# Nine of 49 exponentials on VectorE, taken two at a time, a plan with a lock between VectorE and GpSimd, and another layout for the horizontal results

## The chip, the cores and the metric

The kernel runs on one core of a Trainium2 chip. The metric is the device time of one execution in microseconds. Five engines work side by side, each through a queue of its own in order: TensorE (PE in the profile, PEld for its weight loads), ScalarE (ACT), VectorE (DVE), GpSimd (POOL), and SyncE (SP), whose queue here issues all DMAs. They meet at semaphores.

## The reference

Window attention in two directions on one 224 x 224 image with 96 channels, bfloat16. The first 48 channels attend inside horizontal stripes of 8 rows, the last 48 inside vertical stripes of 8 columns; each stripe is a window of 1792 tokens, and there are 28 + 28 of them. Then one projection of all channels.

```python
def reference(x, wqkv, wo):
    B, H, W, C = x.shape                       # 1, 224, 224, 96
    sw = 8; C2 = C // 2; nh, nw = H // sw, W // sw
    qkv = jnp.einsum('bhwc,cd->bhwd', x, wqkv)
    q, k, v = qkv[..., :C], qkv[..., C:2*C], qkv[..., 2*C:]
    scale = C2 ** (-0.5)
    # horizontal: channels :C2, windows of 8 rows x 224
    ah = softmax(einsum('bqc,bkc->bqk', qh, kh) * scale); oh = einsum('bqk,bkc->bqc', ah, vh)
    # vertical: channels C2:, windows of 224 x 8 columns
    av = softmax(einsum('bqc,bkc->bqk', qv, kv) * scale); ov = einsum('bqk,bkc->bqc', av, vv)
    return jnp.einsum('bhwc,cd->bhwd', concat(oh, ov), wo)
```

## The kernel before

Two windows are done together: a pass `P`. Passes 0 to 13 are horizontal, 14 to 27 vertical. In a pass the 1792 queries are cut into four chunks (512, 512, 512, 256), and each chunk's scores into units of 128 x 1024 (a key tile of 128 by 512 queries by two windows; two key tiles in the chunk of 256). There are 49 units in a pass. For each unit PE makes the scores into one of three PSUM slots of two banks (`qk`, the pool `ring`), an engine makes exponentials of them in SBUF, and PE multiplies these with V and adds them up in one of two further banks (`pv_op`, `obanks`).

- 41 units of a pass go to ScalarE (`add_a`): one `activation` into `PT`, one product with V.
- 8 units go to VectorE (`add_d`; `NDC` says how many of each chunk). Its exponential is built from four instructions of 1024 elements a partition: `I_sb` (the shifted score as int16, the only one that reads PSUM, and it frees the slot), `U_sb` and `E_sb` (fraction and exponent bits, int16 to int16), and `G_sb` (a product of two bf16 tensors). E and G are each multiplied with V, so such a unit has two products.

Around the units, `prep` makes the next pass's K, Q and V from `xT_sb` with `fill`: PE writes a bank, VectorE evicts it. For K the mean over the keys is taken off: VectorE sums it (`kjunk`, `negmean`), and GpSimd subtracts it (`ev3`). When a chunk is complete, VectorE evicts it to `OT_sb` and `fin` projects it: PE, a reciprocal, a product (`d2`). For a horizontal pass `d2` writes `Ph_sb`, which keeps all horizontal results in SBUF. For a vertical pass `d2` writes `tmp`, GpSimd adds `Ph_sb` (`d3`, into `out_sb`), and SP issues one DMA for every 16 x 8 pixels: 28 a pass.

`load` fetches x transposed: 2 DMA transposes for a horizontal pass, 16 of 224 pixels for a vertical one. The load for pass P + 2 goes into the buffer of pass P.

The order is made by a list scheduler (`Planner`) when the kernel is built: each `Op` has an engine, a cost `occ`, a latency, dependencies, buffers to take; each engine has several queues with priorities, and the planner places next what can start first by its costs. What it gives out is a fixed order for every engine, with semaphore waits for the dependencies alone: no start time of the plan is enforced. It reckons 0.06 us of SP's queue for each x load and each output DMA.

Of the kernel before, what the change touches and what calls it, by code (L numbers as in the profile page):

```python
# [218 lines left out]
EPS, HOLD, RUN, BATCH = 0.02, 0.12, 1.5, 2  # L219
PRIO = (1, 0, 3, 5, 4, 2)  # L220
NEAR, LEAD, SPACE, PACE, DRUN = 1, 3, 4, 0.9, 0.9


def bass_standalone__window_attn_cswin__vision_kernel(
# [23 lines left out]
    NPT, NY, NL, NR = 8, 2, 4, 4  # L248

    es = ExitStack()  # L250
    with es:
# [131 lines left out]
        def load(P, stream):  # L383
            b = P % 2
            for w in range(2):
# [10 lines left out]
                for i, (tr, dst, s_) in enumerate(todo):  # L396
                    fn = (lambda e, dst=dst, s_=s_: e.dma_start_transpose(dst, s_)) if tr else \
                         (lambda e, dst=dst, s_=s_: e.dma_start(dst, s_, allow_slow_non_contiguous=True))
                    op = Op("sp", 0.06, 4.0, fn, xt_read.get(P - 2, []) if i == 0 else [], dma=(s_x[b][w], own if i == 0 else 0))
# [162 lines left out]
        ph_ready = {}  # L562
        out_dma = {P: [] for P in range(NP)}

        def fin(P, c):
# [7 lines left out]
            if is_h[P]:  # L573
                bcs = list(range(q0 // 64, (q0 + qs) // 64))
                for i in range(0, len(bcs), 4):
# [16 lines left out]

                    def rel(op, rop=rop):
# [3 lines left out]
                                   ("dve", 0.07 + 0.1 * n, d2, [], True, dve_ev, [], rel)], stream=pe_fin)  # L597
                    rop.append(ops[0])
                    fin_pe[P].append(p)
                    for bc in g:  # L600
                        ph_ready[(P, bc)] = ops[1]
            else:
                kts = list(range(q0 // 128, (q0 + qs) // 128))
                for w in range(2):
                    j = 2 * (P - NPH) + w
                    g, n = kts, len(kts)

                    def pe_fn(e, bk, g=g, n=n, w=w):
# [5 lines left out]
                        return ins
                    hold = []

                    def d2(e, bk, op, n=n, hold=hold):
                        r = rc[hold[0].tok["r"]]
                        return e.tensor_tensor(tmp[op.tok["t"]][:, 0:n, :], bk[:, 0:n * (C + 1)].rearrange("p (s c) -> p s c", s=n)[:, :, 0:C],  # L619
                                               r[:, 0:n].unsqueeze(2).to_broadcast([128, n, C]), ALU.mult)  # L620
# [8 lines left out]
                    def done(op, g=g, w=w, j=j, hold=hold):  # L629
                        tmps.free(hold[1].tok["t"], [op])  # L630
                        for kt in g:
                            dm = Op("sp", 0.06, 2.0, lambda e, kt=kt: e.dma_start(out_v[j, kt], out_sb[b][:, w, kt, :]), [op], dma=(s_out[b], 0))
# [106 lines left out]

        def add_d(u, soft):  # L740
            P, c, kts = u
            b = P % 2
# [7 lines left out]
            d.fn = lambda e: e.tensor_scalar(I_sb[d.tok["y"]][:, :].rearrange("p (s n) -> p s n", s=2), two(q.tok["s"]),  # L750
# [4 lines left out]
            f = Op("dve", 0.334, 0.415, None, [d])  # L755
            f.fn = lambda e: e.tensor_scalar(U_sb[d.tok["y"]][:, :], I_sb[d.tok["y"]][:, :], M_FRAC, HALF, ALU.bitwise_and, ALU.bitwise_or)  # L756
            x2 = Op("dve", 0.334, 0.415, None, [d], [], [(ls, "l", 1)])
            x2.fn = lambda e: e.tensor_scalar(E_sb[x2.tok["l"]][:, :], I_sb[d.tok["y"]][:, :], M_EXP, E_LOW, ALU.bitwise_and, ALU.bitwise_or)  # L758
            g = Op("dve", 0.60, 0.68, None, [f, x2], [], [], lambda op: ys.free(d.tok["y"], [op]))
            g.fn = lambda e: e.tensor_tensor(G_sb[x2.tok["l"]][:, :], I_sb[d.tok["y"]][:, :].bitcast(BF16), U_sb[d.tok["y"]][:, :].bitcast(BF16), ALU.mult)  # L760
            dve_ts.extend([f, x2, g])
            for t, buf in ((x2, E_sb), (g, G_sb)):
                def pv_then(op, t=t):
                    if t is g:
                        ls.free(x2.tok["l"], [op])
                    pv_done(k, op)
                v = pv_op(k, kts, lambda w, kt: V_sb[b][:, w, kt, :],
                          lambda w, i, qs, buf=buf: buf[x2.tok["l"]][:, w * 512 + i * qs:w * 512 + (i + 1) * qs].bitcast(BF16),
                          [t] + v_ready[P], pv_then)
                last_pv[P].append(v)  # L770
                pe_pd.append(v)

        prep(0, startup=True)
# [89 lines left out]
```

## Time and profile before

| | us |
|---|---|
| median of 3 runs (lowest, highest) | 1103.57 (1100.68, 1105.23) |
| the profiled execution | 1103.27 |
| its span, first to last instruction | 1101.5 |
| ACT busy | 1062.8 |
| PE busy | 1046.9 |
| DVE busy | 949.9 |
| POOL busy | 153.3 |

Busy times are unions of what runs on an engine; a matmul's end is modelled, so PE's is no measure of how full it is. The mean time of one instruction in a group is that of its record, and records of neighbours overlap by some hundredths of a microsecond. `L726` and the like are lines of the kernel before. In a timeline the bracket behind a row is the idle time ahead of it and what ended it.

### The profile page before, as it was taken

How to read it: one execution, taken by the hardware profiler on the slowest of the kernel's cores; microseconds unless marked ns; L12 is line 12 of the kernel's file. 1: busy time of each engine (PE TensorE's matmuls, PEld its weight loads, DVE VectorE, ACT ScalarE, POOL GpSimd, SP SyncE). 2: the span in 40 equal slices, each digit the busy share in tenths (PEclk: the TensorE clock that was granted, in tenths of full speed). 3: DMA queues.
4: the chain of work that ended last, by engine and by line, in shares of the span. 5: the costliest groups of instructions: out<-in, count | busy, mean ns of one | idle time of the engine just before them, and what ended most of it. 6: DMA issues, size and time to landing. Idle time of an engine off the chain costs nothing.

```text
span 1101.5 us, 24997 instructions
## 1 busy us (share of the span) xinstructions
PE 1046.9 (95%) x10424; PEld 386.4 (35%) x10424; DVE 949.9 (86%) x1941; ACT 1062.8 (96%) x1154; POOL 153.3 (14%) x143
## 2 busy tenths in 40 slices
PE   7999999999999999999999999999999999989996
PEld 2333333333333333333333333333333333323332
DVE  5899889889888998898899889988988978868876
ACT  4999999999999999999999999999999989979996
POOL 0000000000000000000022122222221222212221
PEclk9999999999999999999999999999999989989998
DMA  5101201110121012011112222222222222222110
GB/s 104 35 1 35 35 9 27 35 35 1 35 35 34 1 35 35 3 33 29 20 29 42 39 41 42 39 41 43 40 41 42 41 39 43 40 39 42 37 29 19
DMA packets 168904, 37.05 MB, mean 34 GB/s; under 512 B 168792, under 2 KB 168792, under 8 KB 168792
## 3 DMA queue, kind: packets, MB, share of 16 engines
q1 hardware_dynamic: 168792, 35.47, 17.5%
q8 instruction: 81, 1.33, 0.5%
q14 instruction: 31, 0.25, 0.1%
HBM read 0.10 MB, written 9.63 MB: 9 GB/s over the span
## 4 chain that ended last, share of the span: by engine, by line
ACT 63%; PE 17%; DVE 17%; issue 1%; DMA 0%; POOL 0%; POOLq 0%; SPq 0%
ACT PT L726 63%; PE ps L708 8%; PE ps L691 7%; DVE I_sb L750 5%; DVE G_sb L760 4%; DVE KT_sb L518 2%; DVE U_sb L756 2%; DVE E_sb L758 1%; DVE OT_sb L655 1%; PE ps L499 1%; PE ps L583 1%; DVE QT_sb L513 1%; DVE Ph_sb L590 1%; DMA xT_sb<-in_x_dram 0%; PE ps L612 0%
## 5 line engine op out<-in xcount | busy, mean ns | idle before, releaser
L726 ACT ACTIVATE PT<-ps 128x1024 bf16<-128x1024 f32 x1148 | 1059.3, 1107 | 20.8 <-PE ps L708 20.1
L708 PE MATMUL ps<-QT_sb,KT_sb 48*128 48x512 bf16 (+1 forms) x3136 | 490.9, 360 | 25.4 <-ACT PT L726 16.0
L691 PE MATMUL ps<-PT,V_sb 128*64 128x512 bf16 (+1 forms) x2576 | 447.6, 371 | 0.3 <-ACT PT L726 0.3
L750 DVE TENSOR_SCALAR I_sb<-ps 128x1024 int16<-128x1024 f32 x224 | 273.4, 1221 | 42.7 <-PE ps L708 37.7
L708 PEld LDWEIGHTS ps<-QT_sb,KT_sb 48*128 48x128 bf16 x3136 | 125.1, 93 | 327.8 <-ACT PT L726 195.6
L691 PEld LDWEIGHTS ps<-PT,V_sb 128*64 128x64 bf16 x2576 | 134.1, 108 | 170.4 <-issue 160.4
L760 DVE TENSOR_TENSOR G_sb<-I_sb,U_sb 128x1024 bf16<-128x1024 bf16 x224 | 176.9, 790 | 3.3
L623 POOL TENSOR_TENSOR out_sb<-tmp,Ph_sb 128x384 bf16<-128x384 f32 (+1 forms) x112 | 99.8, 896 | 414.4 <-DVE tmp L619 338.9
L529 POOL TENSOR_SCALAR KT_sb<-KT_sb,negmean 128x1792 bf16<-128x1792 bf16 x27 | 53.3, 1976 | 529.8 <-DVE kjunk L523 529.7
L756 DVE TENSOR_SCALAR U_sb<-I_sb 128x1024 int16<-128x1024 int16 x224 | 96.5, 431 | 2.0
L691 PE MATMUL ps<-G_sb,V_sb 128*64 128x512 bf16 (+1 forms) x560 | 91.1, 356 | 5.7 <-DVE G_sb L760 4.9
L499 PE MATMUL ps<-xT_sb,w_sb 96*64 96x512 bf16 x448 | 84.4, 379 | 11.1 <-issue 10.8
L758 DVE TENSOR_SCALAR E_sb<-I_sb 128x1024 int16<-128x1024 int16 x224 | 92.7, 414 | 0.0
L691 PE MATMUL ps<-E_sb,V_sb 128*64 128x512 bf16 (+1 forms) x560 | 89.6, 350 | 1.5 <-DVE E_sb L758 0.9
L518 DVE TENSOR_SCALAR_CACHE_REDUCE KT_sb<-ps 128x512 bf16<-128x512 f32 x112 | 68.3, 618 | 22.2 <-PE ps L499 22.0
L555 DVE CAST V_sb<-ps 128x480 bf16<-128x480 f32 x112 | 53.8, 501 | 38.2 <-PE ps L550 37.3
L513 DVE TENSOR_SCALAR QT_sb<-ps 128x512 bf16<-128x512 f32 x108 | 66.9, 619 | 18.2 <-PE ps L499 18.1
L655 DVE CAST OT_sb<-ps 128x512 bf16<-128x512 f32 x112 | 69.3, 618 | 6.8 <-PE ps L691 6.8
L619 DVE TENSOR_TENSOR tmp<-ps,rc 128x384 f32<-128x384 f32 (+1 forms) x112 | 56.3, 502 | 1.0
L590 DVE TENSOR_TENSOR Ph_sb<-ps,rc 128x384 bf16<-128x384 f32 x98 | 54.1, 552 | 0.6
L691 PEld LDWEIGHTS ps<-G_sb,V_sb 128*64 128x64 bf16 x560 | 27.0, 108 | 56.1 <-DVE G_sb L760 39.2
L571 DVE RECIPROCAL rc<-ps 128x4 f32<-128x4 f32 (+1 forms) x210 | 36.3, 173 | 10.3 <-PE ps L612 10.3
(28 smaller groups left out, 281.6 us busy)
## 6 DMA issues: line engine op xcount, KB each, us to landing
out_dram<-out_sb SPq DMA_DIRECT2D x392, 24.0 KB, 1.9
xT_sb<-in_x_dram SPq DMA_TRANSPOSE x252, 2.5
wo_sb<-in_wo_dram SPq DMA_DIRECT2D x4, 9.0 KB
wo_sb<-one_sb SPq DMA_DIRECT2D x4, 0.0 KB
w_sb<-in_wqkv_dram SPq DMA_DIRECT2D x1, 54.0 KB, 2.5
xT_sb<-in_x_dram SPq DMA_DIRECT2D x2, 3.0 KB, 3.9
```

The lines of the kernel that those rows point to most:

```text
L499: ins = e.matmul(bk[64 * w:64 * w + 64, 0:qs], lhsT=w_sb[0:C, wblk(P, kind), :], rhs=rhs, start=True, stop=True)
L513: return e.tensor_scalar(dst, src, A128, None, ALU.mult)
L518: return e.tensor_scalar(KT_sb[b][:, q0:q0 + qs], bk[:, 0:qs], 1.0, None, ALU.mult, ALU.add, accum_out=ksum[b][:, c:c + 1])
L623: return e.tensor_tensor(out_sb[b][:, w, g[0]:g[0] + n, :], tmp[hold[1].tok["t"]][:, 0:n, :], Ph_sb[:, g[0]:g[0] + n, j, :], ALU.add)
L655: return e.tensor_copy(OT_sb[b][:, q0:q0 + qs], bk[:, 0:qs])
L691: ins = e.matmul(bank(k.bank)[64 * w:64 * w + 64, 0:qs], lhsT=lhs(w, kt), rhs=rhs(w, i, qs), start=(op.tok["first"] and i == 0), stop=(k.l ...
L708: ins = e.matmul(bank(2 * s + w)[:, i * qs:(i + 1) * qs], lhsT=KT_sb[b][64 * w:64 * w + C2, kt * 128:(kt + 1) * 128], rhs=QT_sb[b][64 * w: ...
L726: a.fn = lambda e: e.activation(PT[a.tok["p"]][:].rearrange("p (s n) -> p s n", s=2), two(q.tok["s"]), ACTF.Exp, scale=LN128)
L750: d.fn = lambda e: e.tensor_scalar(I_sb[d.tok["y"]][:, :].rearrange("p (s n) -> p s n", s=2), two(q.tok["s"]), 128.0 * ONE, 0.0, ALU.add, ...
L756: f.fn = lambda e: e.tensor_scalar(U_sb[d.tok["y"]][:, :], I_sb[d.tok["y"]][:, :], M_FRAC, HALF, ALU.bitwise_and, ALU.bitwise_or)
L758: x2.fn = lambda e: e.tensor_scalar(E_sb[x2.tok["l"]][:, :], I_sb[d.tok["y"]][:, :], M_EXP, E_LOW, ALU.bitwise_and, ALU.bitwise_or)
L760: g.fn = lambda e: e.tensor_tensor(G_sb[x2.tok["l"]][:, :], I_sb[d.tok["y"]][:, :].bitcast(BF16), U_sb[d.tok["y"]][:, :].bitcast(BF16), AL ...
```

## The change

**Units.** VectorE gets a third unit of the first chunk: nine units a pass, 40 left to ScalarE. VectorE's units go in pairs: two `I_sb` into the halves of one buffer of 2048, one `U_sb` and one `E_sb` of 2048, and two `G_sb` of 1024. When a pair is planned, `choose` may put a `G_sb` on GpSimd: 21 of 252.

**The plan.** An op with `lock` (all of GpSimd's, and VectorE's U, E and G) is planned to start only when the last one with a lock is over. This is a cost in the plan; no semaphore is added for it. SP's costs are now 1.28 us for an x load and 0.64 us for other DMAs. Several constants of the planner change.

**Horizontal results.** `d2` of a horizontal pass writes a staging view of `out_sb`, and eight DMAs a pass carry it to `Ph_sb`, which is now laid out by image row (112 partitions, two halves). A vertical chunk's projection now takes four groups of 112 pixels (two matmuls each, 64 and 48 wide) in place of four (or two) of 128, and one DMA writes it: 8 a pass. The vertical Q is no longer re-ordered while it is evicted.

```diff
-NDC = [2, 2, 2, 2]
+NDC = [3, 2, 2, 2]
 class Op:
...
+        s.lock = eng == "pool"
 class Planner:                     # ready()
+        if op.lock:
+            t = max(t, s.lock)
                                    # place()
+        if op.lock:
+            s.lock = t + op.occ + 0.03
-EPS, HOLD, RUN, BATCH = 0.02, 0.12, 1.5, 2
+EPS, HOLD, RUN, BATCH = 0.05, 0.12, 1.2, 1
-NEAR, LEAD, SPACE, PACE, DRUN = 1, 3, 4, 0.9, 0.9
+WANT = 0.8
+NEAR, LEAD, SPACE, PACE, DRUN = 1, 8, 3, 0.9, 1.0
-    NPT, NY, NL, NR = 8, 2, 4, 4
+    NPT, NY, NL, NR = 8, 2, 3, 4
-        I_sb = [sb(f"I_sb{i}", [128, 1024], I16) for i in range(NY)]
+        I_sb = [sb(f"I_sb{i}", [128, 2048], I16) for i in range(NY)]
...
-        Ph_sb = sb("Ph_sb", [128, NPH, WB, C], BF16)
+        Ph_sb = sb("Ph_sb", [128, 2, 2 * NPH, SW, C], BF16)
                                    # load()
-                    op = Op("sp", 0.06, 4.0, fn, ...
+                    op = Op("sp", 1.28, 4.0, fn, ...
                                    # fin(), horizontal
-                        return e.tensor_tensor(Ph_sb[:, P, g[0]:g[0] + n, :], ...
+                        return e.tensor_tensor(stage(b)[:, g[0]:g[0] + n, :], ...
+                    staged[P].append(ops[1])
+                    if len(staged[P]) == 7:
+                        r0 = 2 * SW * (P % 7)
+                        for dw in range(8):
+                            fn = lambda e, dw=dw: e.dma_start(Ph_sb[r0:r0 + 2 * SW, P // 7, :, dw, :], stage(b)[dw:128:8, :, :])
+                            dm = Op("sp", 0.64, 2.5, fn, staged[P], dma=(s_out[b], 0))
                                    # fin(), vertical
-                        for kt in g:
-                            dm = Op("sp", 0.06, 2.0, lambda e, kt=kt: e.dma_start(out_v[j, kt], out_sb[b][:, w, kt, :]), ...
+                        fn = lambda e: e.dma_start(out_v[:, :, SW * j + 2 * c:SW * j + 2 * c + 2, :]...)
+                        dm = Op("sp", 0.64, 2.0, fn, [op], dma=(s_out[b], 0))
                                    # add_d()
+            f = Op("dve", 0.60, 0.68, None, ds)
+            f.fn = lambda e: e.tensor_scalar(U_sb[y()][:, :], I_sb[y()][:, :], M_FRAC, HALF, ...)
+            x2 = Op("dve", 0.60, 0.68, None, ds, [], [(ls, "l", 1)])
+            f.lock = x2.lock = True
+            for i0, i1 in ((0, 1024), (1024, 2048)):
+                g = Op("dve", 0.62, 0.70, None, [f, x2])
+                g.lock = True
+            def choose(op):
+                work = sum(o_.occ for q_ in (dve_ot, dve_d1, dve_ev) for o_ in q_ if all(d_.end is not None for d_ in o_.deps))
+                for g in gs:
+                    if work >= WANT and pl.t["pool"] <= op.start + 1.0:
+                        work -= WANT
+                        g.eng, g.occ, g.lat = "pool", 2.12, 2.2
```

What stands in the queues of SP, VectorE and GpSimd, before and after:

SP's queue in the vertical half, a pass and a little more of it before (`L397` is the x load, `L632` the output):

```order
L632 DMA out_dram<-out_sb 16x8x96 x24
L397 DMA_TRANSPOSE xT_sb<-in_x_dram 128x1x224 x3
L632 DMA out_dram<-out_sb 16x8x96 x4
L397 DMA_TRANSPOSE xT_sb<-in_x_dram 128x1x224 x13
L632 DMA out_dram<-out_sb 16x8x96 x24
L397 DMA_TRANSPOSE xT_sb<-in_x_dram 128x1x224 x3
```

The same half after (`L408` is the x load, `L656` the output):

```order
L408 DMA_TRANSPOSE xT_sb<-in_x_dram 128x1x224 x9
L656 DMA out_dram<-out_sb 112x2x192 x2
L408 DMA_TRANSPOSE xT_sb<-in_x_dram 128x1x224
L656 DMA out_dram<-out_sb 112x2x192
L408 DMA_TRANSPOSE xT_sb<-in_x_dram 128x1x224 x6
L656 DMA out_dram<-out_sb 112x2x192 x5
L408 DMA_TRANSPOSE xT_sb<-in_x_dram 128x1x224 x5
```

Before, 28 outputs stand between one pass's 16 loads and the next's; now it is 8, spread among the loads.

VectorE in an early horizontal pass, around `kjunk`, which releases GpSimd's subtraction of the K mean; before:

```order
L750 TENSOR_SCALAR I_sb<-ps 128x1024
L523 TENSOR_SCALAR kjunk,negmean<-ksum 128x4
L756 TENSOR_SCALAR U_sb<-I_sb 128x1024
L758 TENSOR_SCALAR E_sb<-I_sb 128x1024
L513 TENSOR_SCALAR QT_sb<-ps 128x512
L760 TENSOR_TENSOR G_sb<-I_sb,U_sb 128x1024
L655 CAST OT_sb<-ps 128x512
L750 TENSOR_SCALAR I_sb<-ps 128x1024
```

After:

```order
L794 TENSOR_SCALAR U_sb<-I_sb 128x2048
L782 TENSOR_SCALAR I_sb<-ps 128x1024
L534 TENSOR_SCALAR kjunk,negmean<-ksum 128x4
L796 TENSOR_SCALAR E_sb<-I_sb 128x2048
L524 TENSOR_SCALAR QT_sb<-ps 128x512
L801 TENSOR_TENSOR G_sb<-I_sb,U_sb 128x1024
L782 TENSOR_SCALAR I_sb<-ps 128x1024
L683 CAST OT_sb<-ps 128x512
L801 TENSOR_TENSOR G_sb<-I_sb,U_sb 128x1024
```

U and E have twice the width and stand half as often; behind `kjunk` there still stand an E and a G.

GpSimd around the first vertical pass, before (`L529` subtracts the K mean, `L623` adds the horizontal result):

```order
L529 TENSOR_SCALAR KT_sb<-KT_sb,negmean 128x1792 x15
L623 TENSOR_TENSOR out_sb<-tmp,Ph_sb 128x384 x6
L623 TENSOR_TENSOR out_sb<-tmp,Ph_sb 128x192 x2
L529 TENSOR_SCALAR KT_sb<-KT_sb,negmean 128x1792
```

After (`L540`, `L647`, and `L801`, the product that VectorE did alone before):

```order
L540 TENSOR_SCALAR KT_sb<-KT_sb,negmean 128x1792 x2
L801 TENSOR_TENSOR G_sb<-I_sb,U_sb 128x1024
L540 TENSOR_SCALAR KT_sb<-KT_sb,negmean 128x1792
L647 TENSOR_TENSOR out_sb<-tmp,Ph_sb 112x2x2x96 x4
L801 TENSOR_TENSOR G_sb<-I_sb,U_sb 128x1024
L647 TENSOR_TENSOR out_sb<-tmp,Ph_sb 112x2x2x96 x2
L540 TENSOR_SCALAR KT_sb<-KT_sb,negmean 128x1792
```

Products of VectorE's pairs now stand in GpSimd's queue ahead of K means and additions.

More of the change, by code (lines that the diff above doesn't have):

```diff
@@ L22 @@
 M_FRAC, M_EXP, HALF, E_LOW = 0x007F, 0x7F80, 0x3F00, 0x0002
-NDC = [2, 2, 2, 2]
+NDC = [3, 2, 2, 2]
 class Op:
-    __slots__ = ("eng", "occ", "lat", "fn", "deps", "soft", "alloc", "then", "wait", "tok", "dma", "mode", "start", "end")
+    __slots__ = ("eng", "occ", "lat", "fn", "deps", "soft", "alloc", "then", "wait", "tok", "dma", "mode", "start", "end", "lock")
     def __init__(s, eng, occ, lat, fn, deps=(), soft=(), alloc=(), then=None, dma=None, mode=None):
@@ L33, in __init__ @@
         s.wait = s.start = s.end = None
-        s.tok, s.dma, s.mode = {}, dma, mode
+        s.tok, s.dma, s.mode, s.lock = {}, dma, mode, eng == "pool"
 class Pool:
@@ L86, in __init__ @@
         s.switches = 0
+        s.lock = 0.0
         s.busy = {e: 0.0 for e in s.t}
@@ L641, in fin, with evs_of @@
                     hold += ops[:2]
                     fin_pe[P].append(p)
+        def evs_of(P, c):
+            return [chunks[(P, i)].evac for i in range(max(0, c - 1), c + 1)]
         def pv_done(k, op):
@@ L738, in add_a @@
             act_of[i] = a
+        n_d = [0]
+        held = []
         def add_d(u, soft):
@@ L754, in add_d @@
             dve_d1.append(d)
[L755 to L771, printed above, removed]
+            if j == 0:
+                return
@@ new lines, in add_d @@
+            held.clear()
+            units = [u_ for u_, _ in pair]
+            ds = [d_ for _, d_ in pair]
+            y = lambda: ds[0].tok["y"]
+            f = Op("dve", 0.60, 0.68, None, ds)
+            f.fn = lambda e: e.tensor_scalar(U_sb[y()][:, :], I_sb[y()][:, :], M_FRAC, HALF, ALU.bitwise_and, ALU.bitwise_or)
+            x2 = Op("dve", 0.60, 0.68, None, ds, [], [(ls, "l", 1)])
+            x2.fn = lambda e: e.tensor_scalar(E_sb[x2.tok["l"]][:, :], I_sb[y()][:, :], M_EXP, E_LOW, ALU.bitwise_and, ALU.bitwise_or)
@@ new lines, in add_d @@
+            f.lock = x2.lock = True
+            gs = []
+            for i0, i1 in ((0, 1024), (1024, 2048)):
+                g = Op("dve", 0.62, 0.70, None, [f, x2])
+                g.fn = lambda e, i0=i0, i1=i1: e.tensor_tensor(G_sb[x2.tok["l"]][:, i0:i1], I_sb[y()][:, i0:i1].bitcast(BF16),
+                                                              U_sb[y()][:, i0:i1].bitcast(BF16), ALU.mult)
+                g.lock = True
+                gs.append(g)
+            gs[1].then = lambda op: ys.free(y(), gs)
@@ new lines, in add_d, with used, pv_then @@
+            x2.then = choose
+            dve_ts.extend([f, x2])
+            users = []
+            def used(op):
+                users.append(op)
+                if len(users) == 4:
+                    ls.free(x2.tok["l"], users)
+            for buf, src in ((E_sb, [x2, x2]), (G_sb, [gs[0], gs[-1]])):
+                for i, (u_, _) in enumerate(pair):
+                    k_ = chunks[u_[:2]]
+                    def pv_then(op, k_=k_):
+                        used(op)
+                        pv_done(k_, op)
+                    v = pv_op(k_, u_[2], lambda w, kt, u_=u_: V_sb[u_[0] % 2][:, w, kt, :],
+                              lambda w, t, qs, buf=buf, i=i: buf[x2.tok["l"]][:, i * 1024 + w * 512 + t * qs:i * 1024 + w * 512 + (t + 1) * qs].bitcast(BF16),
+                              [src[i]] + v_ready[u_[0]], pv_then)
+                    last_pv[u_[0]].append(v)
+                    pe_pd.append(v)
```

98 lines of the change are left out of this document (57 added, 41 removed).

## The prediction

> **What bounds the kernel now.** I read the busy shares and the groups first, then the waits, then stretches of equal passes, and last the timeline of the stretches where ScalarE is not full.
>
> ```profile
> PE 1046.9 (95%) x10424; PEld 386.4 (35%) x10424; DVE 949.9 (86%) x1941; ACT 1062.8 (96%) x1154; POOL 153.3 (14%) x143
> L726 ACT ACTIVATE PT<-ps 128x1024 bf16<-128x1024 f32 x1148 | 1059.3, 1107 | 20.8 <-PE ps L708 20.1
> PEld ps L708 <- ACT PT L726: 195.6, 575, 0.6
> PEld ps L708 <- DVE I_sb L750: 20.1, 76, 0.6
> ```
>
> ScalarE is busy for 96% of the span, with 1059.3 / 1148 = 0.923 us for each unit. PE's 95% says less: its loads for the scores wait 195.6 us in total for ScalarE to free a PSUM slot, so PE is ahead of ScalarE. The next rows give five whole passes of each half (DVE is the third pair of columns, ACT the fourth), then three stretches of 100 us in the vertical half.
>
> ```profile
> 108.91:298.63 189.72, 183.56 (x1862) 69.16 (x1860) 167.92 (x341) 188.72 (x205) 10.88 (x5) 1.00 0.14 26
> 654.72:843.48 188.76, 183.92 (x1862) 67.07 (x1862) 169.96 (x351) 188.68 (x206) 44.22 (x45) 1.00 0.22 41
> 740.00:840.00 100.00, 97.61 (x954) 34.99 (x954) 90.13 (x189) 99.97 (x110) 23.57 (x24) 1.00 0.22 41
> 840.00:940.00 100.00, 94.42 (x952) 34.52 (x948) 85.27 (x174) 94.65 (x103) 21.45 (x22) 0.97 0.21 40
> 940.00:1040.00 100.00, 94.44 (x894) 33.34 (x894) 83.49 (x175) 93.60 (x102) 22.38 (x23) 0.95 0.22 40
> ```
>
> A horizontal pass takes 189.72 / 5 = 37.94 us, a vertical one 188.76 / 5 = 37.75, and ScalarE idles for 0.2 and 0.0 us of it. VectorE works 33.58 and 33.99 us and idles 4.36 and 3.76. From 840 to 1040 us ScalarE loses 5.3 + 6.4 = 11.7 us, and the granted clock (the column of 1.00, 0.97, 0.95) falls. The timeline shows on what:
>
> ```profile
> 663.61 3.93 SPq L397 DMA_TRANSPOSE xT_sb<-in_x_dram  x3
> 667.59 2.51 SPq L632 DMA_DIRECT2D out_dram<-out_sb  x4
> 670.14 17.12 SPq L397 DMA_TRANSPOSE xT_sb<-in_x_dram  x13
> 687.31 16.65 SPq L632 DMA_DIRECT2D out_dram<-out_sb  x24
> 704.06 3.75 SPq L397 DMA_TRANSPOSE xT_sb<-in_x_dram  x3
> ...
> 892.66 0.41 PE L499 MATMUL ps<-xT_sb,w_sb 96*64 96x512 bf16 x2 [2.30 <-issue]
> 893.66 1.94 ACT L726 ACTIVATE PT<-ps 128x1024 bf16<-128x1024 f32 x2 [2.24 <-PE ps L708]
> 933.96 0.41 PE L499 MATMUL ps<-xT_sb,w_sb 96*64 96x512 bf16 x2 [0.96 <-issue]
> 974.85 0.41 PE L499 MATMUL ps<-xT_sb,w_sb 96*64 96x512 bf16 x2 [3.14 <-issue]
> ...
> 894.00:895.00 1.00, 1.00 (x6) 0.16 (x6) 0.78 (x3) 1.00 (x2) 0.00 (x0) 0.50 0.21 41
> 900.00:901.00 1.00, 1.00 (x10) 0.46 (x8) 0.52 (x3) 0.67 (x1) 0.00 (x0) 0.69 0.26 49
> 901.00:902.00 1.00, 1.00 (x16) 0.49 (x12) 1.00 (x5) 0.25 (x1) 0.00 (x0) 1.00 0.16 33
> ```
>
> SP's queue is a second bound that grows in secret. From 663.61 to 704.06 it needs 40.45 us for one pass's 16 x loads and 28 outputs, with no gap, while a pass takes 37.75: it falls behind by 2.7 us a pass. At 890 us the loads are late enough that PE's first projection of x (L499) stops for 2.30 us, later for 0.96 and 3.14 us ("issue" here, since the wait is on a DMA). Behind the gap of 2.30 us the granted clock is 0.50 from 894 to 900 us, and ScalarE loses more than the gap.
>
> **The change, part by part.**
>
> *ScalarE's units.* 28 x 0.923 = 25.8 us less work, all on the path, and a pass's floor goes from 41 to 40 units: 40 x 37.75 / 41 = 36.83 us.
>
> *SP.* A vertical pass now has 16 loads of 17.12 / 13 = 1.32 us and 8 outputs of 2.51 / 4 = 0.63: 26.1 us of 36.8, so the queue no longer falls behind, and the late loads go: 11.7 us. They stand in one queue with outputs that wait for GpSimd, but 10 us a pass are free for that. A horizontal pass gets eight DMAs more (5.0 us) beside two loads; only the additions of vertical passes wait for these, and the last eight once, at the middle of the run, off ScalarE's path. What is late next is VectorE.
>
> *VectorE.* These rows price it (the last four are single instructions, of one horizontal pass and of the start):
>
> ```profile
> L750 DVE TENSOR_SCALAR I_sb<-ps 128x1024 int16<-128x1024 f32 x224 | 273.4, 1221 | 42.7 <-PE ps L708 37.7
> L760 DVE TENSOR_TENSOR G_sb<-I_sb,U_sb 128x1024 bf16<-128x1024 bf16 x224 | 176.9, 790 | 3.3
> L756 DVE TENSOR_SCALAR U_sb<-I_sb 128x1024 int16<-128x1024 int16 x224 | 96.5, 431 | 2.0
> L758 DVE TENSOR_SCALAR E_sb<-I_sb 128x1024 int16<-128x1024 int16 x224 | 92.7, 414 | 0.0
> L619 DVE TENSOR_TENSOR tmp<-ps,rc 128x384 f32<-128x384 f32 x84 | 46.4, 553 | 0.9
> L619 DVE TENSOR_TENSOR tmp<-ps,rc 128x192 f32<-128x192 f32 x28 | 9.8, 351 | 0.1
> 12.38 0.69 DVE L528 TENSOR_SCALAR KT_sb<-KT_sb,negmean 128x1792 bf16<-128x1792 bf16 x1
> 216.10 0.68 DVE L760 TENSOR_TENSOR G_sb<-I_sb,U_sb 128x1024 bf16<-128x1024 bf16 x1
> 218.43 2.17 POOL L529 TENSOR_SCALAR KT_sb<-KT_sb,negmean 128x1792 bf16<-128x1792 bf16 x1 [35.77 <-DVE kjunk L523]
> 219.61 1.53 DVE L760 TENSOR_TENSOR G_sb<-I_sb,U_sb 128x1024 bf16<-128x1024 bf16 x1
> ```
>
> I: 28 more at 1.22 = +34.2 us. G: 231 in place of 224 at 0.79 = +5.6. U and E: 448 of 1024 (189.2 us) become 252 of 2048. No row has 2048; the nearest, 1792 elements (L528), took 0.69, and twice the row of 1024 is 0.86, so these are the ends; on the line through 431 ns at 1024 and 0.69 us at 1792 it is 0.77, which I take: 252 x 0.77 = 194, +4.8 (ends -15 and +28). The vertical projections: all 112 products are now of four groups, where 28 had two: an extra 28 x (0.553 - 0.351) = +5.6. Sum +50 us of records (ends +30 and +74). Records overlap: VectorE's groups add up to about 1063 where the union is 949.9, a factor of 0.89, so busy time rises by some 45 us (27 to 66), or 1.6 us a pass (1.0 to 2.4): 35.2 and 35.6 us of 36.83. VectorE is then 96% full. Before it was 89% full, and ScalarE lost 0.2 us a horizontal pass. I let that double, and the vertical passes get the same 0.2: 28 x 0.2 = +5.6 us.
>
> The Trainium skill, "VectorE: DVE Perf Modes", section "The perf-mode tier table", gives 693 ns for a tensor_scalar of 2048 bf16 elements in SBUF. By that the U and E term would be 252 x 0.693 = 175, -15 in place of +4.8, the lower end of mine. No row here shows that size.
>
> *The lock.* G alone takes 0.68 us, and 1.53 beside GpSimd's K mean: that overlap costs VectorE 0.85 us. The plan wants to avoid it, but there is no wait behind it. In the order before, 27 of 28 `kjunk` and 47 of 112 `tmp` products are followed by a U, E or G that starts (by the trace's durations) while GpSimd still works; after, it is 24 and 47. So I put the gain at nothing; its ends are -28 x 0.85 = -24 us of VectorE's time, and for the 21 G on GpSimd, each able to hold VectorE up likewise, +18 us.
>
> *PE* gets 28 more products with V, two matmuls each (and loses the wait for 28 activations); hidden behind its 195.6 us of waits. The Q eviction writes as many elements as before. *The end*: behind ScalarE's last unit the last projection is of four groups and not two, but two DMAs go out and not four; I take these as equal.
>
> *Sum*: 1101.5 - 25.8 - 11.7 + 5.6 = 1069.6 us of span. The profiled execution took 1103.27, 1.8 us more than its span, and lies 0.3 us under the median of 1103.57; so 1071.4, and 1071 is my forecast.
>
> **The rivals.** The first three are points of one scale: how much of VectorE's idle time (4.06 us a pass on average) stays when it gets 1.6 us more work. It runs in order, and its idle time is waits for PE:
>
> ```profile
> DVE I_sb L750 <- PE ps L708: 37.7, 90, 3.3
> DVE V_sb L555 <- PE ps L550: 37.3, 28, 1.6
> ```
>
> If they are only because VectorE is early, they shrink as it fills. There is room for 36.83 - 35.4 = 1.4 us a pass, a third of them; up to there ScalarE sets the pass (my forecast).
>
> 1. *VectorE becomes the bound.* Half of its idle time stays: 35.4 + 2.0 = 37.43 us a pass, against 37.85 before; 28 x 0.42 = 11.8 and the 11.7 of the loads: 1103.3 - 23.5 = 1080. At 65% it is 38.04, and 1097. For it: both ends of the lock's term and the 21 products in GpSimd's queue. Against it: in the rows above, V's 37.3 us are one wait in each of 28 passes of at most 1.6 us, for a PE that is itself paced by ScalarE.
> 2. *Slower: all of it stays*, because a pair makes stretches of U, E and G, twice as long, that hold the queue while PSUM slots wait for their I. A pass is then 35.4 + 4.06 = 39.5 us, 1.65 more than 37.85: 1103.3 - 11.7 + 46 = 1138. It decides from the point where 2.9 of the 4.06 us stay, since then a pass loses what the loads win. Against it: PE waits 20.1 us in 76 waits for the slots that I frees, a tenth of what it waits for ScalarE's.
> 3. *VectorE has more room than I think* (2048 at 0.69 us, the lock works): no further loss, and the 0.2 us of the horizontal passes go as well: 1060 to 1063.
> 4. *SP stays late.* The outputs are spread among the loads and wait for GpSimd, so the loads behind them come as late as before: only the 25.8 us are won, 1103.3 - 25.8 + 5.6 = 1083. Against it: 26 us of work in 36.8.
>
> The Trainium skill, "SBUF — State Buffer", section "Who interferes with whom", says that VectorE and GpSimd share a port pair under an exclusive lock: a VectorE instruction with two SBUF inputs is blocked whole by a GpSimd instruction that reads SBUF. The 0.68 and 1.53 us of G agree. By that rule the 21 products on GpSimd work against the change, as rival 1 has it.
>
> **How the numbers follow.** Forecast (with rival 3 on its low side) 0.68, rival 1 0.15, rival 2 0.08, rival 4 0.09. The range reaches down to 1058, a little under rival 3, and up to 1094, nearly the whole of rival 1, which leaves out rival 2 and the tails. The forecast's own range is 1060 to 1079. A measurement of this kernel tells 0.5% (5.5 us) from no change. Faster by that: the forecast, rival 4 and most of rival 1, 0.89; within it 0.04, from rival 1 near 65% and beyond; slower 0.07.
>
> **What would show it.** In the profile after: 1120 activations at 0.92 us; ScalarE's idle time before L726's successor near 15 us, and no waits of over 1 us ahead of x's projection; SP with gaps in every vertical pass; granted clock 1.00 from start to end. VectorE between 975 and 1015 us busy, U and E between 0.69 and 0.86 us each; G still above 0.75 us on average if the lock does nothing. A horizontal pass near 37.0 to 37.2 us. I am wrong if the passes take 37.5 us or more with VectorE full, or if PE stops for x again.

## The result, and the profile after

The changed kernel takes 1059.22 us (median of four runs, 1059.0 to 1060.41) against 1104.4 us of the kernel before in the same rounds: a ratio of 0.959, with a 95% interval of 0.956 to 0.963. The forecast was 1071, its range 1058 to 1094. The profiled execution took 1060.41 us, its span is 1058.6.

From the page of the kernel after: the busy shares, the chain that ended last by engine, and the main groups (busy us, mean ns | idle us ahead of them):

```profile
PE 1031.1 (97%) x10592; PEld 385.3 (36%) x10592; DVE 967.4 (91%) x1780; ACT 1032.0 (97%) x1126; POOL 221.6 (21%) x164
ACT 94%; PE 4%; DMA 1%; DVE 0%; issue 0%; SPq 0%; ACTq 0%; POOL 0%; POOLq 0%
L754 ACT ACTIVATE PT<-ps 128x1024 bf16<-128x1024 f32 x1120 | 1028.6, 1261 | 9.8 <-PE ps L736 8.0
L782 DVE TENSOR_SCALAR I_sb<-ps 128x1024 int16<-128x1024 f32 x252 | 307.2, 1219 | 29.2 <-PE ps L736 26.2
L801 DVE TENSOR_TENSOR G_sb<-I_sb,U_sb 128x1024 bf16<-128x1024 bf16 x231 | 167.8, 733 | 0.2
L794 DVE TENSOR_SCALAR U_sb<-I_sb 128x2048 int16<-128x2048 int16 x126 | 87.6, 695 | 0.6
L796 DVE TENSOR_SCALAR E_sb<-I_sb 128x2048 int16<-128x2048 int16 x126 | 85.9, 681 | 0.0
L801 POOL TENSOR_TENSOR G_sb<-I_sb,U_sb 128x1024 bf16<-128x1024 bf16 x21 | 45.0, 2146 | 117.2 <-DVE E_sb L796 117.2
```

Two of its waits (us in total, times, longest):

```profile
PEld ps L736 <- ACT PT L754: 279.4, 830, 0.8
ACT PT L754 <- PE ps L736: 8.0, 13, 1.4
```

ScalarE is the bound and hardly waits. The chain is 94% ScalarE, and PE's waits for a slot that ScalarE frees have grown from 195.6 to 279.4 us. Before, the chain ran through the other engines far more often, 17% of it through VectorE:

```profile
ACT 63%; PE 17%; DVE 17%; issue 1%; DMA 0%; POOL 0%; POOLq 0%; SPq 0%
```

Of the 42.9 us that the span lost, ScalarE's units hold 1059.3 - 1028.6 = 30.7, and its waits 20.8 - 9.8 = 11.0. (A unit's pace is read as busy time over count, 1028.6 / 1120 = 0.918 us. The mean record of 1261 ns is longer, since the records of neighbouring activations overlap by far more than those of VectorE.)

Two of its windows (VectorE is the third column pair, ScalarE the fourth):

```profile
200.00:400.00 200.00, 197.32 (x2028) 75.19 (x2026) 188.29 (x342) 200.00 (x220) 17.26 (x8) 1.00 0.33 46
900.00:1000.00 100.00, 98.76 (x1012) 36.20 (x1010) 94.38 (x178) 99.75 (x110) 36.69 (x27) 1.00 0.18 36
```

Its timeline, of ScalarE and then of SP:

```profile
32.36 1.02 ACT L754 ACTIVATE PT<-ps 128x1024 bf16<-128x1024 f32 x1 [0.94 <-PE ps L736]
...
38.75 660.10 ACT L754 ACTIVATE PT<-ps 128x1024 bf16<-128x1024 f32 x720 [0.47 <-PE ps L736]
699.09 122.94 ACT L754 ACTIVATE PT<-ps 128x1024 bf16<-128x1024 f32 x134 [0.23 <-PE ps L736]
823.38 228.84 ACT L754 ACTIVATE PT<-ps 128x1024 bf16<-128x1024 f32 x249 [1.36 <-PE ps L719]
...
693.42 7.54 SPq L408 DMA_TRANSPOSE xT_sb<-in_x_dram  x6
709.75 2.92 SPq L656 DMA_DIRECT2D out_dram<-out_sb  x4
714.05 11.42 SPq L408 DMA_TRANSPOSE xT_sb<-in_x_dram  x9
```

From 38.75 us to the end ScalarE stops visibly only twice, for 0.23 and 1.36 us. In the first stretch 720 units take 660.10 us, so a pass of 40 takes 36.67. VectorE is 94% full. SP has gaps (8.8 us between the first two of its rows), no x load stops PE after the start, and the granted clock is 1.00 in every window up to 1000 us.

### The profile page after: what moved, and what is told of

Read it like the earlier page. It is cut to its first block, busy times and chain, and to the rows that moved or that the text cites. A ratio compares the mean times of both kernels' runs of the same rounds, so it can differ in the third digit from the quotient of the medians.

```text
span 1058.6 us, 24969 instructions
## 1 busy us (share of the span) xinstructions
PE 1031.1 (97%) x10592; PEld 385.3 (36%) x10592; DVE 967.4 (91%) x1780; ACT 1032.0 (97%) x1126; POOL 221.6 (21%) x164
## 3 DMA queue, kind: packets, MB, share of 16 engines
q8 instruction: 83, 1.36, 0.6%
## 4 chain that ended last, share of the span: by engine, by line
ACT 94%; PE 4%; DMA 1%; DVE 0%; issue 0%; SPq 0%; ACTq 0%; POOL 0%; POOLq 0%
ACT PT L754 94%; PE ps L736 2%; PE ps L719 2%; PE ps L510 1%; DMA xT_sb<-in_x_dram 1%; PE ps L561 0%; SPq L408 0%; PE ps L634 0%; DVE OT_sb L683 0%; ACTq L257 0%; POOL out_sb L647 0%; POOLq L257 0%; ACT QT_sb L523 0%; DVE tmp L643 0%; DVE wo_sb L369 0%
## 5 line engine op out<-in xcount | busy, mean ns | idle before, releaser
L754 ACT ACTIVATE PT<-ps 128x1024 bf16<-128x1024 f32 x1120 | 1028.6, 1261 | 9.8 <-PE ps L736 8.0
L719 PE MATMUL ps<-PT,V_sb 128*64 128x512 bf16 (+1 forms) x2520 | 393.5, 367 | 0.7 <-ACT PT L754 0.7
L782 DVE TENSOR_SCALAR I_sb<-ps 128x1024 int16<-128x1024 f32 x252 | 307.2, 1219 | 29.2 <-PE ps L736 26.2
L736 PEld LDWEIGHTS ps<-QT_sb,KT_sb 48*128 48x128 bf16 x3136 | 130.2, 93 | 359.1 <-ACT PT L754 279.4
L647 POOL TENSOR_TENSOR out_sb<-tmp,Ph_sb 112x384 bf16<-112x384 f32 x112 | 120.9, 1092 | 274.6 <-DVE tmp L643 223.0
L801 DVE TENSOR_TENSOR G_sb<-I_sb,U_sb 128x1024 bf16<-128x1024 bf16 x231 | 167.8, 733 | 0.2
L540 POOL TENSOR_SCALAR KT_sb<-KT_sb,negmean 128x1792 bf16<-128x1792 bf16 x27 | 55.8, 2068 | 442.6 <-DVE kjunk L534 437.5
L794 DVE TENSOR_SCALAR U_sb<-I_sb 128x2048 int16<-128x2048 int16 x126 | 87.6, 695 | 0.6
L796 DVE TENSOR_SCALAR E_sb<-I_sb 128x2048 int16<-128x2048 int16 x126 | 85.9, 681 | 0.0
L529 DVE TENSOR_SCALAR_CACHE_REDUCE KT_sb<-ps 128x512 bf16<-128x512 f32 x112 | 68.8, 617 | 15.6 <-PE ps L510 15.3
L801 POOL TENSOR_TENSOR G_sb<-I_sb,U_sb 128x1024 bf16<-128x1024 bf16 x21 | 45.0, 2146 | 117.2 <-DVE E_sb L796 117.2
L643 DVE TENSOR_TENSOR tmp<-ps,rc 112x384 f32<-112x384 f32 x112 | 61.8, 552 | 1.6
L606 DVE TENSOR_TENSOR out_sb<-ps,rc 128x384 bf16<-128x384 f32 x98 | 54.0, 551 | 1.1
L561 PE MATMUL ps<-w_sb,xT_sb 96*64 96x48 bf16 x1568 | 44.5, 192 | 0.0
```

Of the source, the lines that this page charges most:

```text
L529: return e.tensor_scalar(KT_sb[b][:, q0:q0 + qs], bk[:, 0:qs], 1.0, None, ALU.mult, ALU.add, accum_out=ksum[b][:, c:c + 1])
L647: return e.tensor_tensor(out_sb[b][0:HB, :, w, 2 * c:2 * c + 2, :].rearrange("p h d c -> p d h c"), tmp[hold[1].tok["t"]][0:HB, 0:n, :].re ...
L719: ins = e.matmul(bank(k.bank)[64 * w:64 * w + 64, 0:qs], lhsT=lhs(w, kt), rhs=rhs(w, i, qs), start=(op.tok["first"] and i == 0), stop=(k.l ...
L736: ins = e.matmul(bank(2 * s + w)[:, i * qs:(i + 1) * qs], lhsT=KT_sb[b][64 * w:64 * w + C2, kt * 128:(kt + 1) * 128], rhs=QT_sb[b][64 * w: ...
L754: a.fn = lambda e: e.activation(PT[a.tok["p"]][:].rearrange("p (s n) -> p s n", s=2), two(q.tok["s"]), ACTF.Exp, scale=LN128)
L782: d.fn = lambda e: e.tensor_scalar(I_sb[d0.tok["y"]][:, j * 1024:(j + 1) * 1024].rearrange("p (s n) -> p s n", s=2), two(q.tok["s"]), 128. ...
```

## The experiments

The kernel before ran beside them at 1105.4, 1107.5 and 1105.5 us. Theory: the forecast's three terms (ScalarE's units, SP, and a VectorE for which the lock does nothing). Rival: the change lives by its plan, which keeps VectorE apart from GpSimd.

**SP alone: the kernel before with 8 of 28 output DMAs in a vertical pass.** The other 20 outputs of a pass are left out.

```diff
-                        for kt in g:
+                        for kt in g[:1]:
```

> The kernel before, with 8 of the 28 output DMAs of a vertical pass issued (20 of 28 pieces of the result are not written). If SP's full queue makes the x loads late, the 11.7 us that ScalarE loses from 840 to 1040 us go, with the clock at 1.00: 1092 us (1090 to 1094). Rival, the projections of x stop for another reason (the DMA engines' share, the additions): it stays at 1101 to 1106.

Measured: 1089.51 us (ratio 0.981 to 0.986). ScalarE's group, then two windows:

```profile
L726 ACT ACTIVATE PT<-ps 128x1024 bf16<-128x1024 f32 x1148 | 1057.8, 1105 | 10.3 <-PE ps L708 10.1
```

```profile
800.00:900.00 100.00, 97.31 (x1018) 36.19 (x1016) 90.47 (x188) 99.95 (x110) 22.62 (x24) 1.00 0.16 31
900.00:1000.00 100.00, 97.23 (x988) 34.91 (x986) 88.76 (x182) 99.95 (x110) 23.52 (x24) 1.00 0.16 29
```

ScalarE is full to the end, and 15.9 us are won, 4 us more than the 11.7 expected; the time lies half a microsecond under the expected range.

**The other way: the changed kernel with each output DMA cut in four, 32 a pass.**

```diff
-    fn = lambda e: e.dma_start(out_v[:, :, SW * j + 2 * c:...], out_sb[b][0:HB, ...])
+    for r in range(0, HB, 28):
+        fn = lambda e, r=r: e.dma_start(out_v[r:r + 28, :, SW * j + 2 * c:...], out_sb[b][r:r + 28, ...])
```

> The changed kernel with each output DMA cut into four of 28 partitions: 32 a vertical pass, so SP has 16 x 1.32 + 32 x 0.63 = 41.3 us of work in 36.7. Theory: SP falls behind by 4.6 us a pass, the x loads get late after some four to five passes, PE stops ahead of x's projection and the clock falls: 1090 to 1115. Rival, the layout and not the number of DMAs took the stop away: 1059 to 1063.

Measured: 1115.62 us (1.0045 to 1.0104 of before), just over the theory's range. Two windows, then a stretch of the timeline (SP, and ScalarE at its end):

```profile
100.00:200.00 100.00, 98.60 (x1022) 37.13 (x1022) 94.58 (x175) 100.00 (x110) 8.62 (x4) 1.00 0.35 41
800.00:900.00 100.00, 89.18 (x876) 34.13 (x874) 82.95 (x155) 79.86 (x87) 23.05 (x21) 0.88 0.20 39
```

```profile
770.00 14.85 SPq L657 DMA_DIRECT2D out_dram<-out_sb  x24
784.89 1.10 SPq L408 DMA_TRANSPOSE xT_sb<-in_x_dram  x1
786.63 6.45 SPq L657 DMA_DIRECT2D out_dram<-out_sb  x12
...
807.64 1.94 ACT L755 ACTIVATE PT<-ps 128x1024 bf16<-128x1024 f32 x2 [6.03 <-PE ps L737]
```

The horizontal half is untouched and the vertical one loses 56 us; in the worse window ScalarE is at 80% and the clock at 0.88. SP has gaps even so, and so does not fall behind by the expected 4.6 us a pass. Loads stand behind groups of outputs in its queue, and the order was planned anew for this run: the run shows that the number of outputs brings the stops back, not how much of that is the queue's fill and how much its order.

**Nine units on the old code**, with SP as it was, and with 8 outputs a pass (the others left out).

```diff
-NDC = [2, 2, 2, 2]
+NDC = [3, 2, 2, 2]
```

> The kernel before with nine units a pass for VectorE and nothing else of the change. Theory: the horizontal half wins 14 x 0.92 = 13 us; the vertical half wins little, since SP's 40.5 us a pass are now 3.7 over a pass and not 2.7, so the loads are late sooner: 1088 to 1098. Rival, VectorE is the bound without pairs: horizontal passes stay at 37.5 us or more, and 1100 or over. If neither bites: 1078.

> The kernel before with nine units in the first block of K, and 8 of 28 output transfers in each vertical pass (the rest of the outputs are left out). Theory (without pairs and lock VectorE paces the horizontal half at 37.6 us a pass, so SP's freedom gives back the late loads alone): 1082-1090, ScalarE's idle still above 20 us. Rival (the units count in full once SP is free, so pairs and lock are not needed): 1060-1070.

Measured: 1099.65 (0.992 to 0.997), between theory and rival, and 1083.79 us (0.976 to 0.983), as the theory had it. A horizontal window of the second:

```profile
200.00:400.00 200.00, 191.80 (x1990) 72.95 (x1988) 189.83 (x386) 196.08 (x214) 8.79 (x5) 1.00 0.16 28
```

The ninth unit wins 5.7 us of 25.8 with either queue (1105.4 - 1099.65, 1089.51 - 1083.79; by its interval 3 to 8.5), and a free SP 15.9 with either count: these two add up. VectorE is 95% full here and ScalarE 98%, so on the old order ScalarE does not set the pass alone.

**Eight and ten units in the new code**, and eight with the planner's old constants.

```diff
-NDC = [3, 2, 2, 2]
+NDC = [2, 2, 2, 2]     # eight; with the old constants also: EPS 0.02, RUN 1.5, BATCH 2, LEAD 3, SPACE 4, DRUN 0.9
+NDC = [3, 3, 2, 2]     # ten
```

> The changed kernel with eight units a pass for VectorE, 41 for ScalarE. Theory, ScalarE alone sets the pass: 28 x 0.917 = 25.7 us more, 1085 (1083 to 1088). Rival, VectorE holds back the changed kernel too, and is relieved here: under 1080.

> The changed kernel with eight units in every block of K and the planner's constants of before. Theory (the units of ScalarE count in full: 28 x 0.918 = 25.7 us, and pairs and lock alone give back the late loads and the gap in each pass): 1080-1090. Rival (eight units leave a wait at the end of each pass whatever the constants, as in the run of eight units that took 1101): 1095-1105.

> The changed kernel with ten units a pass for VectorE, 39 for ScalarE. Theory, VectorE at 34.5 us of a pass has no room for another 2.3 us: a pass of 36.8 us or more with VectorE over 97% busy, 1060 to 1075. Rival, it still waits only because it is early, and ScalarE still sets the pass: 1034.

Measured: 1100.84 (0.9915 to 0.9957), 1105.27 (0.998 to 1.0015) and 1114.05 us (1.005 to 1.010). ScalarE's timeline with eight (1100.84), in a horizontal and a vertical pass:

```profile
228.98 37.69 ACT L754 ACTIVATE PT<-ps 128x1024 bf16<-128x1024 f32 x41 [0.26 <-PE ps L736]
...
804.30 8.36 ACT L754 ACTIVATE PT<-ps 128x1024 bf16<-128x1024 f32 x9 [0.28 <-PE ps L736]
813.14 29.49 ACT L754 ACTIVATE PT<-ps 128x1024 bf16<-128x1024 f32 x32 [0.49 <-PE ps L736]
```

Busy shares and ScalarE's group with ten:

```profile
PE 1054.2 (95%) x10648; PEld 389.0 (35%) x10648; DVE 1021.9 (92%) x1824; ACT 1016.0 (91%) x1098; POOL 317.7 (29%) x204
L754 ACT ACTIVATE PT<-ps 128x1024 bf16<-128x1024 f32 x1092 | 1012.6, 1138 | 78.7 <-PE ps L719 41.2
```

Eight with the old constants came out at the upper edge of its rival; the other two runs missed theory and rival both. With ten, ScalarE waits 78.7 us, and no engine is full: VectorE is 92% busy and not the 97% expected. Its plan sends 61 products to GpSimd, and U is stretched again:

```profile
L794 DVE TENSOR_SCALAR U_sb<-I_sb 128x2048 int16<-128x2048 int16 x140 | 108.1, 772 | 0.3
```

So that VectorE's work alone bounds this run is not shown. With eight (1100.84), ScalarE waits in every pass at the same place, though VectorE is only 84% busy (82% with the old constants). So eight in the new code (1101, 1105) are worse than eight in the old with a free SP (1090): the new order brings nothing for them. Why the eight wait was not found; that the waits repeat to 0.01 us from pass to pass points to the order.

**The lock.** The same kernel, planned without it. The order on the engines differs, and with it what `choose` gives to GpSimd: 31 products and not 21.

```diff
-        s.tok, s.dma, s.mode, s.lock = {}, dma, mode, eng == "pool"
+        s.tok, s.dma, s.mode, s.lock = {}, dma, mode, False
-            f.lock = x2.lock = True
-                g.lock = True
```

> The changed kernel with no op locked in the plan. Theory, the lock is not enforced and moves nothing that ScalarE waits for: 1058 to 1062, G on VectorE 0.73 to 0.79 us on average. Rival, the lock is what gave VectorE its room: G over 0.80 us, VectorE over 985 us busy, 1065 or more.

Measured: 1105.08 us (0.995 to 1.0006 of before): the whole gain is gone (its ten runs lie between 1095 and 1110), and the forecast's "nothing" for the lock with it. VectorE's G and E, and GpSimd's products:

```profile
L800 DVE TENSOR_TENSOR G_sb<-I_sb,U_sb 128x1024 bf16<-128x1024 bf16 x221 | 183.6, 846 | 0.4
L796 DVE TENSOR_SCALAR E_sb<-I_sb 128x2048 int16<-128x2048 int16 x126 | 96.5, 766 | 0.0
L800 POOL TENSOR_TENSOR G_sb<-I_sb,U_sb 128x1024 bf16<-128x1024 bf16 x31 | 66.6, 2150 | 340.5 <-DVE E_sb L796 340.5
```

A horizontal window, and one place of the timeline in order of time:

```profile
200.00:400.00 200.00, 188.68 (x1960) 72.62 (x1958) 184.12 (x323) 192.97 (x210) 21.26 (x10) 0.99 0.32 42
...
306.88 2.13 POOL L540 TENSOR_SCALAR KT_sb<-KT_sb,negmean 128x1792 bf16<-128x1792 bf16 x1 [11.76 <-DVE kjunk L534]
307.39 2.16 DVE L796 TENSOR_SCALAR E_sb<-I_sb 128x2048 int16<-128x2048 int16 x1
309.48 0.67 DVE L683 CAST OT_sb<-ps 128x512 bf16<-128x512 f32 x1
310.21 0.62 PE L719 MATMUL ps<-E_sb,V_sb 128*64 128x512 bf16 x4 [1.25 <-DVE OT_sb L683]
311.19 1.02 ACT L754 ACTIVATE PT<-ps 128x1024 bf16<-128x1024 f32 x1 [0.85 <-PE ps L736]
```

Read downward: GpSimd subtracts the K mean for 2.13 us; an E that takes 0.68 alone starts inside it and lasts 2.16; the eviction of an output bank stands behind it on VectorE; PE waits 1.25 us for that bank, and ScalarE 0.85 us for PE.

Counted over the two traces, a U, E or G of VectorE shares time with 30 of GpSimd's 31 products without the lock, and with 6 of 21 with it. For the K means it is 27 and 20 of 27, for the final sums 44 and 47 of 112. So what the lock keeps apart is above all the products; most K means still meet one.

**Is it GpSimd's running time, or the order?** GpSimd's operations cut short, once without and once with the lock, the order kept. Left out: all but 64 of 1792 columns in the subtraction of K's mean, 88 of 96 channels of the final sums from the third vertical pass on, and all but 64 of GpSimd's G columns from the second pass on.

```diff
-  tensor_scalar(KT_sb[b][:, :], KT_sb[b][:, :], negmean[b][:, 0:1], ...)
+  tensor_scalar(KT_sb[b][:, 0:64], KT_sb[b][:, 0:64], negmean[b][:, 0:1], ...)
```

> The kernel without the lock in the plan (1105 us), with GpSimd's three kinds of operation cut short: the subtraction of K's mean on 64 of 1792 columns, the sums of the horizontal and vertical results on 8 of 96 channels from the third vertical pass on, and G's on 64 of 1024 columns from the second pass on; those results are left out, the order on every engine is kept. Theory (the loss without the lock is the running time of VectorE's operations beside GpSimd's): G's mean falls from 846 ns to below 720, E's from 766 to near 690, VectorE's busy time from 996 us to below 970, ScalarE's idle from 46 us to near 10, and the time to 1058-1068. Rival (the loss is in the order alone, GpSimd's share of the ports is nothing): G stays above 0.80 us or the time stays above 1095.

> The changed kernel with the same three cuts on GpSimd (those results are left out; order kept). Theory (with the lock, ScalarE waits for nothing, so VectorE's time is not on the path): 1056-1060, within 0.5% of the changed kernel, though VectorE's busy time falls by some 5-25 us from 967. Rival (what is left of contention still costs ScalarE its last waits and its slower pace): below 1053.

Measured: 1064.36 us without the lock (0.9575 to 0.965), 1058.76 with it (0.953 to 0.961), both as the theory had it. Two groups and a window without the lock:

```profile
L802 DVE TENSOR_TENSOR G_sb<-I_sb,U_sb 128x1024 bf16<-128x1024 bf16 x221 | 148.5, 687 | 0.4
L796 DVE TENSOR_SCALAR E_sb<-I_sb 128x2048 int16<-128x2048 int16 x126 | 85.7, 680 | 0.0
```

```profile
200.00:400.00 200.00, 194.67 (x2036) 75.23 (x2028) 183.62 (x337) 198.84 (x217) 5.28 (x11) 1.00 0.35 47
```

Busy shares and G with the lock:

```profile
PE 1029.9 (97%) x10592; PEld 384.7 (36%) x10592; DVE 955.8 (90%) x1780; ACT 1031.9 (98%) x1126; POOL 90.7 (9%) x164
L803 DVE TENSOR_TENSOR G_sb<-I_sb,U_sb 128x1024 bf16<-128x1024 bf16 x231 | 156.6, 684 | 0.2
```

The same order, freed of GpSimd's running time, wins 40.7 of the 45.9 us that the lost lock costs: most of that cost is GpSimd's running time, and about 5 us are the order. Late results of GpSimd are not the way: without the lock PE's waits for them add up to 0.9 us in the whole run. So it is VectorE's stretched instructions. How much of the 45.9 us comes from the ten more products that GpSimd gets without the lock was not tried. With the lock the overlap that is left (11.6 us of VectorE's busy time) costs next to nothing (1059.22 against 1058.76).

**The pairs, and the constants.** VectorE's units one by one, as before (nine of them, none on GpSimd, with the lock); and the changed kernel with the planner's constants of before.

```diff
-    NPT, NY, NL, NR = 8, 2, 3, 4
+    NPT, NY, NL, NR = 8, 2, 4, 4            # one by one: I, U, E, G of 1024 each
-EPS, HOLD, RUN, BATCH = 0.05, 0.12, 1.2, 1
-NEAR, LEAD, SPACE, PACE, DRUN = 1, 8, 3, 0.9, 1.0
+EPS, HOLD, RUN, BATCH = 0.02, 0.12, 1.5, 2  # old constants
+NEAR, LEAD, SPACE, PACE, DRUN = 1, 3, 4, 0.9, 0.9
```

> The changed kernel with VectorE's units taken one by one as before (U, E, G of 1024 each, none on GpSimd), nine a pass. U and E at 0.43 and 0.41 are 213 us in place of 174, and 21 G come back: some 35 us of records more, 1.1 us a pass after overlap, to 35.6 of 36.7 us. Theory, ScalarE starves somewhat: 1062 to 1075. Rival, pairs are not needed for nine units: 1057 to 1061.

> The changed kernel with the planner's constants of before (EPS, HOLD, RUN, BATCH, LEAD, SPACE, DRUN). Theory, the constants give the plan in which ScalarE loses nothing in a pass: with the old ones the gap of 0.2 us and the pace of 0.920 us a unit come back, 1064 to 1070. Rival, the plan around them decides nothing: 1058 to 1061.

Measured: 1071.55 us (0.965 to 0.971) one by one, as expected; 1088.26 (0.979 to 0.986) with the old constants, 18 us over the theory's range. Busy shares and ScalarE's group, one by one:

```profile
PE 1040.5 (97%) x10592; PEld 382.9 (36%) x10592; DVE 992.8 (93%) x2053; ACT 1034.2 (97%) x1126; POOL 173.7 (16%) x143
L754 ACT ACTIVATE PT<-ps 128x1024 bf16<-128x1024 f32 x1120 | 1030.8, 1214 | 18.6 <-PE ps L736 11.0
```

The same with the old constants:

```profile
PE 1026.6 (95%) x10592; PEld 382.6 (35%) x10592; DVE 966.7 (89%) x1783; ACT 1036.1 (95%) x1126; POOL 212.6 (20%) x161
L754 ACT ACTIVATE PT<-ps 128x1024 bf16<-128x1024 f32 x1120 | 1032.6, 1161 | 30.4 <-PE ps L736 19.8
```

Pairs, with the 21 products on GpSimd that come with them, are worth 12.3 us, the constants 29.0. With the old constants VectorE is as busy as in the changed kernel (966.7 and 967.4 us), and ScalarE waits 30.4 us in place of 9.8. Which constant does it was not tried. These prices do not add up: 12.3, 29.0 and the lock's 45.9 are 87 us, about twice the whole gain. Each says what the finished plan loses when that one part is taken out.

## Why the prediction was right, and where it was not

The total was near, 12 us high, and the mechanism that it names holds: ScalarE stays the bound, and SP is freed. In span 42.9 us went where 31.9 were forecast. Of the 11.0 between them, 4.9 are ScalarE's pace, 4.9 its waits (11.0 went, 11.7 - 5.6 = 6.1 were forecast), and 1.2 lie elsewhere. But that the sum came so near is in part luck: it puts the lock at nothing, and without the lock the kernel takes 1105 us.

- *SP, 11.7 us*: right in kind, and low by 1.5 to 4 us. The pair with 8 and 28 outputs shows 15.9 against the median, 13.2 in span (1101.5 to 1088.3): 10.5 of waits (20.8 to 10.3), 1.5 of busy time, 1.2 elsewhere.
- *28 units by 0.923, all on the path*: right for the whole change only. On the old code they bring 5.7 us. The other 24.6 of the way from 1083.79 to 1059.22 come with the rest of the change: 12.2 down to the new code with units one by one (1071.55), 12.3 from there with pairs. The 12.2 hold the lock, the constants, SP's new costs in the plan and the new layout of the horizontal results; the last two have no run of their own. The price of a unit that leaves is what it can bring, and the order decides how much of it arrives.
- *+5.6 us for a tighter VectorE*: wrong, there is no such loss. The 0.2 us that ScalarE idled in each horizontal pass went as well, and its pace went from 0.923 to 0.918 us a unit (4.9 us on 1120). In ScalarE's rows above, a unit by itself lasts 1.02 us and 134 in a row take 122.94, 0.917 each, so each stop costs about 0.10 us beside itself. The timeline shows 34 uninterrupted stretches before and 14 after; these account for 2 us of the 4.9. The rest is in stops too short for the timeline: from one unit's end to the next it is 915 to 920 ns in 983 of 1147 cases before and in 1098 of 1119 after, and 920 to 1100 ns in 75 and 2.
- *VectorE's busy time, 995 us*: 28 too high. U and E of 2048 took 695 and 681 ns, not 770: (770 - 688) x 252 = 21 us of records. G fell to 733 ns from the 790 that I carried over: 231 x 0.057 = 13. Times the factor of 0.89 that is 30. The Trainium skill, "VectorE: DVE Perf Modes", section "The perf-mode tier table", has 693 ns for 2048 bf16 elements. The int16 rows here, 695 and 681 ns, agree.
- *The lock at nothing*: wrong, by 46 us of total time. The sum carries over G's 790 ns from the old order; the new order without the lock has 846, and 766 for E. I counted how many U, E or G stand behind a `kjunk`, 24 of 28, and did not ask which ones they are, who waits behind them, or what meets the products on GpSimd. The count for the kernel before, 27 of 28, was too high as well: in its trace a U, E or G shares time with 16 of GpSimd's 27 K means. From 100 to 600 us (the horizontal half and a little of the vertical) the minimum, median and maximum in the changed kernel are:

```profile
L801 DVE TENSOR_TENSOR G_sb<-I_sb,U_sb x117: 656/681/1560, 103.3 to 597.5; 128x1024 bf16<-128x1024 bf16 x117
L796 DVE TENSOR_SCALAR E_sb<-I_sb x62: 658/682/690, 101.9 to 595.8; 128x2048 int16<-128x2048 int16 x62
L794 DVE TENSOR_SCALAR U_sb<-I_sb x61: 661/685/693, 105.9 to 595.2; 128x2048 int16<-128x2048 int16 x61
```

No U or E is stretched there, only some G. The same rows without the lock reach 1973, 2164 and 1664 ns.

- *Rivals 1 and 2* (VectorE's waits stay) come nearest to what happens without the lock: VectorE busy for 995.8 us, my number, and 1105 us, between rival 1's 1097 and rival 2's 1138. *Rival 3* (2048 at 0.69 us, the lock works, the 0.2 us go) is what happened, and its 1060 to 1063 were 1 us too high. Of these only the upper end follows from its terms (1071.4 - 5.6 - 14 x 0.2 = 1063). *Rival 4* did not come: the loads stand free.
- *The model of VectorE's idle time* is what failed beneath it. Busy for 992.8 us it gives 1071.55 (units one by one, with lock), for 995.8 us 1105 (pairs, no lock), and for 966.7 us 1088 (old constants). The sum of an engine's work does not say how long PE and ScalarE wait; one instruction of 2.16 us ahead of an eviction can decide it.
- *The signs to look for*: ScalarE's idle 9.8 us (15 forecast), a horizontal pass 36.67 us (37.0 to 37.2), VectorE 967.4 us busy (975 to 1015), clock 1.00, no late x load. G's 733 ns lie under the 0.75 us named for a lock that does nothing.

## What to carry to other kernels

Before VectorE gets more work, ask which of its instructions can meet one of GpSimd's, and what stands in the queue behind each: here an order alone, without a wait, kept many of them apart, and the kernel planned without it took 46 us more. An SP queue whose issues take longer than a pass falls behind unseen and shows up many passes later as a late load, so add up its rows per pass. The work that leaves the bounding engine is no gain yet: change the count and the plan apart, and look at the plan again for each count. Here what served nine units fitted neither eight nor ten.

## What the runs showed of the hardware

- An E has one SBUF input and was stretched all the same, 0.68 to 2.16 us, while the PSUM reads (`I_sb`) lay between 1.205 and 1.226 us in the same stretch of the kernel without the lock. The prediction had named only instructions with two inputs. The Trainium skill, "SBUF — State Buffer", section "SBUF: two separate sides", counts instructions in a two-port performance mode among the blocked ones too. The stretched E agrees with that if it runs in such a mode; no run here shows the mode itself.
- With almost nothing to do, GpSimd's subtraction of K's mean still takes 628 ns (64 columns, in the run with the lock and GpSimd cut short), against 2068 ns on 1792 in the changed kernel:

```profile
L540 POOL TENSOR_SCALAR KT_sb<-KT_sb,negmean 128x64 bf16<-128x64 bf16 x27 | 17.0, 628 | 476.2 <-DVE kjunk L534 469.3
```

```profile
L540 POOL TENSOR_SCALAR KT_sb<-KT_sb,negmean 128x1792 bf16<-128x1792 bf16 x27 | 55.8, 2068 | 442.6 <-DVE kjunk L534 437.5
```
